# Moving the constants and pools of a float32r attention and feed-forward kernel so that TensorE's operands start at multiples of 128 bytes

## The chip, the cores and the metric

The kernel runs on one core of a Trainium2 chip. A core has five engines with queues of their own: TensorE (in the profile PE, with its weight loads as PEld), VectorE (DVE), ScalarE (ACT), GpSimd (POOL) and SyncE (SP). They share a memory of 128 partitions; a tile is a block of bytes at one offset in each of its partitions. TensorE multiplies a stationary operand (the weights, loaded by LDWEIGHTS) with a moving operand that is streamed column by column; both are read from this memory, and the product goes to the accumulators (PSUM). The metric is the device time in microseconds of one execution.

## The reference

Windowed causal attention over 8 batches of 8 heads, 576 positions, 64 elements each, and a feed-forward layer with a leaky activation on its output (4608 tokens, 512 -> 2048 -> 512), all in float32:

```python
rel = pos[:, None] - pos[None, :]
mask = (rel >= 0) & (rel < 64)
scores = np.where(mask, scale * np.matmul(q, k.transpose(0, 1, 3, 2)), -1000000000.0)
attn = np.exp(scores - np.max(scores, axis=-1, keepdims=True))
attn = attn / (np.sum(attn, axis=-1, keepdims=True) + 1e-09)
x = np.matmul(attn, v)          # then heads side by side: (4608, 512)
h = x @ w_in
g = np.maximum(h, 0.0) + alpha * np.minimum(h, 0.0)
return g @ w_out
```

The weights of the layer come as float64.

## The kernel before

Tokens are worked in 36 tiles of 128, in 13 blocks (`SIZES`: three of two tiles, ten of three). Per tile, attention computes scores (`s`, L490, full float32), a masked minimum and exponentials (DVE L504, ACT L512), a normalisation (POOL L529), a transpose (TensorE L553 in the opening, DVE L545 and L547 later) and the values (`av`, L577). The values are split into a high part `xh` and a low part `xl`, both of the type float32r (four bytes).

The layer runs in cells. Cell (n, f) is one block n and one slice f of 128 of the 2048 hidden features, 16 cells per block. `m_hidden` (L708 to L718) makes the hidden product from three split products of four matmuls each: `win_h` with `xh`, `win_h` with `xl`, `win_l` with `xh`. The weights are stationary; `xh` or `xl` moves, 384 columns wide in a block of three tiles and 256 in a block of two. Then come the slopes (ACT L724), the larger (DVE L730), the high part `gh` (ACT L737) and the low part `gl` (POOL L744). `m_add` (L749 to L762) adds to the output of each tile of the block: `gh` with `wout_h`, `gl` with `wout_h`, `gh` with `wout_l`. Here `gh` or `gl` is stationary (128 columns), and `wout_h` or `wout_l` moves, 512 columns wide. `o` of a cell is issued `LAG` = 2 cells after its `h`. So a cell of a three-tile block is 12 matmuls of 384 columns and 9 of 512.

The first three blocks are run by an order that `list_schedule` makes from estimated durations in `opening_graph`, because in that time the weights are still loaded and converted from float64 into high and low parts (DVE L389 to L416, ACT L394 and L433, POOL L422 and L437). From block 3 on the order is written out (L870 to L884), with attention for later blocks mixed in at two places of a block, for nine blocks (`attention_of`, called for blocks 3 to 11).

Nothing in either order depends on where a tile lies. Tiles are placed in the memory pool by pool in the order in which the pools are made (`const`, `io`, `wk`, `gp`), and inside `const` in the order of the calls of `const.tile`, each rounded up to 32 bytes. The first 1152 bytes of a partition (9 x 128) are taken before that. In `const` there stand first `ident` (512 bytes), `masks` (1536), `ebias` (4, rounded to 32), `alpha_rows` (512), `s_sb`, `s20_sb`, `s52_sb` (64 each), `ebias20` (32) and `sa_sb` (64): together 2880 bytes, 22.5 x 128. So `win_h` starts at byte 4032, 64 past a multiple of 128, and since `win_h` and all that follows it in `const` (`win_l`, `wout_h`, `wout_l`, two `pt`, `xh`, `xl`, `v`, `k`), in `io` (`raw`, `exp`, `val`) and at the head of `wk` (two `q`, two `w`) is a whole multiple of 128 long, they all start there: `wout_h` at 69568, `xh` at 143296, `w` at 206784. At the end of `wk` stand six small tiles of 32 bytes, 192 together, so that `gp` starts at 215168, a multiple of 128, and with it all of `g`, `gh` and `gl`. `ident` does too. Slices of these tiles that TensorE reads are offset by multiples of 128 bytes.

Of the kernel before, what the change touches and what calls it, by code (L numbers as in the profile page):

```python
# [9 lines left out]
F32 = mybir.dt.float32  # L10
F32R = mybir.dt.float32r
# [7 lines left out]
RING = 6  # L19
# [8 lines left out]
KRING = 3  # L28
# [144 lines left out]
def list_schedule(ops, slots, favour):  # L173
# [86 lines left out]
    v=(-24, -15, -188), vl=(26, -57, 103), xh=(211, 94, 23), xl=(-44, -6, 99),  # L260
# [26 lines left out]
def banded_attention_then_prelu_ffn(  # L287
# [15 lines left out]
    P = 128  # L303
    D = 64
    W = WINDOW
    KW = 2 * W
    C, T = qT.shape[0] * P, qT.shape[2] * P
    DFF = w_in.shape[1] // 2
    E = w_out.shape[1] // 2
    NP = C // P  # L310
    NF = DFF // P
# [8 lines left out]

    const = ctx.enter_context(tc.tile_pool(name="const", bufs=1))
    io = ctx.enter_context(tc.tile_pool(name="io", bufs=2))
    wk = ctx.enter_context(tc.tile_pool(name="wk", bufs=2))
    gp = ctx.enter_context(tc.tile_pool(name="gp", bufs=3))
    ps_o = ctx.enter_context(tc.tile_pool(name="ps_o", bufs=3, space=PSUM))
    ps_h = ctx.enter_context(tc.tile_pool(name="ps_h", bufs=2, space=PSUM))
    ps_a = ctx.enter_context(tc.tile_pool(name="ps_a", bufs=3, space=PSUM))


    ident = const.tile([P, P], F32, name="ident")  # L330
    nc.gpsimd.memset(ident, 1.0)
# [11 lines left out]

    for h in range(2):
        nc.gpsimd.memset(masks[h * W:(h + 1) * W, 1 + h, 0:W], NEG)
    ebias = const.tile([P, 1], F32, name="ebias")
    nc.vector.memset(ebias, -896.0 * 2**23)


# [7 lines left out]
    nc.vector.memset(ebias20, -916.0 * 2**23)  # L357
    sa_sb = const.tile([P, NF], F32, name="sa_sb")

    win_h = const.tile([P, NP, DFF], F32R, name="win_h")  # L360
    win_l = const.tile([P, NP, DFF], F32R, name="win_l")
    wout_h = const.tile([P, NF, E], F32R, name="wout_h")
    wout_l = const.tile([P, NF, E], F32R, name="wout_l")

# [71 lines left out]


    st = {}  # L440
    pts = [const.tile([P, 2, 2, 2, 2, W], F32, name=f"pt_{i}") for i in range(2)]
    xh = const.tile([P, NP, RING * P], F32R, name="xh")
    xl = const.tile([P, NP, RING * P], F32R, name="xl")
    tiles = [(n, i) for n, ts in enumerate(blocks) for i, t in enumerate(ts)]

    vring = const.tile([P, 2, 2 * KRING + 1, P], F32, name="v")
    kring = const.tile([P, 2, 2 * KRING + 1, 2, W], F32, name="k")

    def of_tile(t, name, shape):
        d = st.setdefault(t, {})  # L450
# [475 lines left out]
```

## Time and profile before

| | |
|---|---|
| median of the runs (3) | 921.17 us |
| lowest, highest | 920.11, 921.48 us |
| the profiled execution, its own time | 919.93 us |
| its span, first to last instruction | 917.9 us |
| granted TensorE clock over the span | 0.999 |
| bytes read from and written to the chip's main memory | 48.24 MB, 9.44 MB |

The page's second part, the span in 40 slices of 23 us, shows how the work is spread: the first row is TensorE, the others the engines that convert the weights and then accompany the cells; each digit is the busy share in tenths.

```profile
PE   9989999999999999999999999999999999999998
DVE  6999965236556455454454454454454445441111
ACT  6997767343453543543443443444344344332322
POOL 4899982233233332332333333333233233232221
```

The first six slices are the opening; after them DVE, ACT and POOL are half idle. The profile's durations of matmuls overlap: a matmul of 512 columns is listed with 397 ns (mean), while the next one starts well before that. Where the distance between matmuls matters, it has to be read from the starts in the timeline. Attribution of waits is inferred from semaphores.

### The profile page before, as it was taken

Reading aid. Unit: us, or ns where it says so; the run is one execution under the profiler, and the core shown is the slowest. Engines: PE = TensorE matmul, PEld = TensorE weight load, DVE = VectorE, ACT = ScalarE, POOL = GpSimd, SP = SyncE. Lnnn points to the kernel's source line nnn. Section 1 sums busy time; section 2 is a strip of 40 time slices with the busy share of each in tenths; the row PEclk is TensorE's granted clock in tenths of the full one; section 3 lists DMA queues with packets and bytes.
Section 4 is the critical chain, followed back from the end, with each engine's and each line's share of the span. In section 5 each row is a group of like instructions: output and inputs, shape, how many; then the busy total and the mean of one; then the engine's idle time right before and its main releaser. Section 6 shows DMA issues by size and latency. Waiting matters only on the chain.

```text
span 917.9 us, 18632 instructions
## 1 busy us (share of the span) xinstructions
PE 907.0 (99%) x7297; PEld 816.8 (89%) x7297; DVE 467.5 (51%) x1508; ACT 424.4 (46%) x1197; POOL 347.5 (38%) x350
## 2 busy tenths in 40 slices
PE   9989999999999999999999999999999999999998
PEld 8878888989999999999999999999999999999997
DVE  6999965236556455454454454454454445441111
ACT  6997767343453543543443443444344344332322
POOL 4899982233233332332333333333233233232221
PEclk9999999999999999999999999999999999999999
DMA  8655524020222013011110210210211200000000
GB/s 269 221 168 164 169 82 127 24 76 1 65 87 64 1 53 98 2 52 60 40 52 35 65 53 35 64 53 35 64 47 42 64 1 24 36 1 1 35 1 34
DMA packets 45606, 58.86 MB, mean 64 GB/s; under 512 B 2880, under 2 KB 38992, under 8 KB 45520
## 3 DMA queue, kind: packets, MB, share of 16 engines
q1 hardware_dynamic: 45056, 57.29, 19.6%
q8 instruction: 57, 0.93, 0.4%
q10 hardware_dynamic: 464, 0.40, 0.1%
q14 instruction: 29, 0.24, 0.1%
HBM read 48.24 MB, written 9.44 MB: 63 GB/s over the span
## 4 chain that ended last, share of the span: by engine, by line
PE 89%; DVE 6%; ACT 1%; issue 1%; POOL 1%; DMA 1%; DVEq 0%; ACTq 0%; POOLq 0%
PE h L717 40%; PE o L759 40%; PE s L490 4%; PE av L577 3%; DVE val L416 1%; DVE man L399 1%; PE warm L831 1%; DVE two L389 1%; DMA raw<-w_in 1%; DVE exp L410 1%; DVE w L504 1%; DVE g L730 1%; PE t L553 0%; POOL val L422 0%; ACT w L512 0%
## 5 line engine op out<-in xcount | busy, mean ns | idle before, releaser
L744 POOL TENSOR_TENSOR gl<-g,gh 128x384 fp32r<-128x384 f32 (+1 forms) x208 | 197.9, 952 | 507.9 <-ACT gh L737 444.0
L730 DVE SCALAR_TENSOR_TENSOR g<-h,s_sb,g 128x384 f32<-128x384 f32 (+1 forms) x208 | 121.9, 586 | 364.4 <-ACT g L724 364.2
L724 ACT ACTIVATE g<-h,sa_sb 128x384 f32<-128x384 f32 (+1 forms) x208 | 115.8, 557 | 324.9 <-PE h L717 320.1
L759 PE MATMUL o<-wout_h,gh 128*128 128x512 f32 x576 | 228.1, 397 | 0.5 <-ACT gh L737 0.4
L759 PE MATMUL o<-wout_h,gl 128*128 128x512 f32 x576 | 227.3, 395 | 0.5 <-POOL gl L744 0.5
L759 PE MATMUL o<-wout_l,gh 128*128 128x512 f32 x576 | 224.2, 390 | 0.0
L717 PE MATMUL h<-xh,win_h 128*128 128x384 f32 (+1 forms) x832 | 171.8, 328 | 3.1 <-DVE exp L410 1.9
L717 PE MATMUL h<-xl,win_h 128*128 128x384 f32 (+1 forms) x832 | 169.1, 324 | 0.0
L717 PE MATMUL h<-xh,win_l 128*128 128x384 f32 (+1 forms) x832 | 168.1, 323 | 0.0
L717 PEld LDWEIGHTS h<-xh,win_h 128*128 128x128 f32 x832 | 142.6, 188 | 22.4 <-DVE exp L410 4.0
L737 ACT CAST gh<-g 128x384 fp32r<-128x384 f32 (+1 forms) x208 | 101.6, 488 | 128.6 <-DVE g L730 116.3
L717 PEld LDWEIGHTS h<-xl,win_h 128*128 128x128 f32 x832 | 143.0, 188 | 0.2 <-DVE rc L521 0.2
L717 PEld LDWEIGHTS h<-xh,win_l 128*128 128x128 f32 x832 | 139.6, 188 | 0.2 <-issue 0.2
L759 PEld LDWEIGHTS o<-wout_l,gh 128*128 128x128 f32 x576 | 108.1, 188 | 23.7
L759 PEld LDWEIGHTS o<-wout_h,gh 128*128 128x128 f32 x576 | 107.9, 188 | 19.8 <-ACT xh L592 1.2
L759 PEld LDWEIGHTS o<-wout_h,gl 128*128 128x128 f32 x576 | 108.3, 188 | 15.9 <-POOL gl L744 1.2
L512 ACT ACTIVATE w<-w,nm 128x128 f32<-128x128 f32 x288 | 112.8, 394 | 5.2 <-DVE nm L504 5.0
L545 DVE STREAM_TRANSPOSE pt<-w 32x256 f32<-32x256 f32 x216 | 94.1, 436 | 5.9 <-POOL w L529 2.9
L529 POOL TENSOR_TENSOR w<-w,rc 128x512 f32<-128x512 f32 x65 | 66.5, 1042 | 48.4 <-DVE rc L521 33.1
L504 DVE CUSTOM_DVE_ANT_0 w<-s,masks 128x128 f32<-128x128 f32 x288 | 64.8, 285 | 7.1 <-PE s L490 7.1
L547 DVE STREAM_TRANSPOSE pt<-w 32x128 f32<-32x128 f32 x216 | 65.4, 303 | 4.2
L512 ACT ACTIVATION_READ_ACCUMULATOR w<-w,nm 128x1 f32 x288 | 54.4, 189 | 0.0
(52 smaller groups left out, 556.5 us busy)
## 6 DMA issues: line engine op xcount, KB each, us to landing
q<-qT SPq DMA_DIRECT2D x35, 256.0 KB, 3.5
out<-os SPq DMA_DIRECT2D x35, 256.0 KB, 2.2
raw<-w_in SPq DMA_DIRECT2D x16, 512.0 KB, 3.8
raw<-w_out SPq DMA_DIRECT2D x16, 512.0 KB, 3.5
k<-kT SPq DMA_DIRECT2D x24, 256.0 KB, 4.5
v<-vN SPq DMA_DIRECT2D x24, 256.0 KB, 4.2
v<-vN SPq DMA_DIRECT2D x12, 384.0 KB, 4.5
k<-kT SPq DMA_DIRECT2D x11, 384.0 KB, 4.4
```

Source lines behind the costliest of these rows:

```text
L490: nc.tensor.matmul(d["s"][a][x][us, 2 * a + h], q[r, a, h, us], kring[r, a, at + u:at + u + 2, h, :], start=True, stop=True)
L504: nc.vector.tensor_tensor_reduce(out=of_head(d["w"], g), in0=d["s"][e // 2][x][:, e].rearrange("p (b k) -> p b k", b=2), in1=mask.rearrang ...
L512: nc.scalar.activation(w, w, AF.Exp, scale=-1.0, bias=d["nm"][:, g:g + 1], accum_out=d["sm"][:, g:g + 1])
L529: nc.gpsimd.tensor_tensor(out=w, in0=w, in1=rc.unsqueeze(1).unsqueeze(3).broadcast_to(list(w.shape)), op=ALU.mult)
L545: nc.vector.transpose(to, w[:, x, j])
L547: nc.vector.transpose(to[:, :, j ^ 1], w[:, x, j, :, j ^ 1])
L717: nc.tensor.matmul(gs[n, f][:, :nt], wt[:, c, fs], xt[:, c, xs], start=(k == 0 and c == 0), stop=(k == 2 and c == NP - 1))
L724: nc.scalar.activation(g, ph[:, :nt], AF.Copy, scale=sa_sb[:, f:f + 1])
L730: nc.vector.scalar_tensor_tensor(out=g, in0=ph[:, :nt], scalar=s_sb[:, f:f + 1], in1=g, op0=ALU.mult, op1=ALU.max)
L737: nc.scalar.copy(gh, gs[n, f])
L744: nc.gpsimd.tensor_tensor(out=gl, in0=g, in1=gh.bitcast(F32), op=ALU.subtract)
L759: nc.tensor.matmul(po[t], g[of_g][:, ts], wt[:, f, :], start=(f == 0 and k == 0), stop=(f == NF - 1 and k == 2))
```

## The change

The large constants are allocated first in `const`, so that `win_h` starts at byte 1152 and each of the following at a multiple of 128; `ident` and `masks` come after them, at multiples of 128 too. `ebias` is made 24 elements long (96 bytes), of which the first is used, as before: with it `const` is 64 bytes longer, and `io` starts at 182272 = 1424 x 128. The pool `gp` is made ahead of `wk`, so that it starts at 202752 (a multiple of 128) and `wk` at 215040, with `q` and `w` at multiples of 128 and its small tiles last. What TensorE reads then lies at a multiple of 128 bytes; `alpha_rows` alone, read by one matmul, starts at 181472, 96 past one. Everything ends at byte 227520 of a partition, 64 further than before. No instruction is added, left out or reordered.

```diff
     const = ctx.enter_context(tc.tile_pool(name="const", bufs=1))
     io = ctx.enter_context(tc.tile_pool(name="io", bufs=2))
+    gp = ctx.enter_context(tc.tile_pool(name="gp", bufs=3))
     wk = ctx.enter_context(tc.tile_pool(name="wk", bufs=2))
-    gp = ctx.enter_context(tc.tile_pool(name="gp", bufs=3))
...
+    win_h = const.tile([P, NP, DFF], F32R, name="win_h")
+    win_l = const.tile([P, NP, DFF], F32R, name="win_l")
+    wout_h = const.tile([P, NF, E], F32R, name="wout_h")
+    wout_l = const.tile([P, NF, E], F32R, name="wout_l")
+    pts = [const.tile([P, 2, 2, 2, 2, W], F32, name=f"pt_{i}") for i in range(2)]
+    xh = const.tile([P, NP, RING * P], F32R, name="xh")
+    xl = const.tile([P, NP, RING * P], F32R, name="xl")
+    vring = const.tile([P, 2, 2 * KRING + 1, P], F32, name="v")
+    kring = const.tile([P, 2, 2 * KRING + 1, 2, W], F32, name="k")
 
     ident = const.tile([P, P], F32, name="ident")
...
-    ebias = const.tile([P, 1], F32, name="ebias")
+    ebias = const.tile([P, 24], F32, name="ebias")[:, :1]
     nc.vector.memset(ebias, -896.0 * 2**23)
...
-    win_h = const.tile([P, NP, DFF], F32R, name="win_h")
-    win_l = const.tile([P, NP, DFF], F32R, name="win_l")
-    wout_h = const.tile([P, NF, E], F32R, name="wout_h")
-    wout_l = const.tile([P, NF, E], F32R, name="wout_l")
...
-    pts = [const.tile([P, 2, 2, 2, 2, W], F32, name=f"pt_{i}") for i in range(2)]
-    xh = const.tile([P, NP, RING * P], F32R, name="xh")
-    xl = const.tile([P, NP, RING * P], F32R, name="xl")
...
-    vring = const.tile([P, 2, 2 * KRING + 1, P], F32, name="v")
-    kring = const.tile([P, 2, 2 * KRING + 1, 2, W], F32, name="k")
```

## The prediction

> **What bounds the kernel.** I read the page first: the span, the busy shares, the chain of work that ended last.
>
> ```profile
> span 917.9 us, 18632 instructions
> PE 907.0 (99%) x7297; PEld 816.8 (89%) x7297; DVE 467.5 (51%) x1508; ACT 424.4 (46%) x1197; POOL 347.5 (38%) x350
> PE 89%; DVE 6%; ACT 1%; issue 1%; POOL 1%; DMA 1%; DVEq 0%; ACTq 0%; POOLq 0%
> ```
>
> TensorE is busy 99% of the span and carries 89% of the chain; no other engine is above 51%. But a busy TensorE says nothing of how fast its matmuls follow each other, and the 6% of DVE lies somewhere. So I asked for the last conversion of the weights (the low parts, L437), and for the busy time on either side of its end.
>
> ```profile
> L437 POOL TENSOR_TENSOR wout_l<-val,wout_h x16: 1287/1299/1326, 25.8 to 130.6; 128x512 fp32r<-128x512 f32 x16
> 132.00:917.90 785.90, 781.79 (x6094) 707.42 (x6092) 352.34 (x1207) 321.17 (x923) 233.86 (x235) 1.00 0.14 44
> ```
>
> The second row's columns are the window, its length, then busy time and count of PE, PEld, DVE, ACT, POOL, then granted clock, DMA share, GB/s. The last low part starts at 130.6 us and takes 1.3, so the weights are all there at 132 us. From then on TensorE is busy for 781.8 of 785.9 us at a granted clock of 1.00. There is no wait to remove after 132 us: only shorter matmuls make that stretch shorter. Before it, the conversions on DVE and POOL set the pace as much as TensorE does.
>
> Next, the distance from one matmul to the next. The durations in the groups (397 ns for a 512-column one) are latencies that overlap, so I took starts from the timeline of TensorE: a cell near the end, a cell of the 256-column blocks, and the 27 `o` matmuls of the tail (first and last).
>
> ```profile
> 851.43 0.87 PE L717 MATMUL h<-xh,win_h 128*128 128x384 f32 x4
> 852.13 0.86 PE L717 MATMUL h<-xl,win_h 128*128 128x384 f32 x4
> 852.84 0.86 PE L717 MATMUL h<-xh,win_l 128*128 128x384 f32 x4
> 853.53 0.39 PE L759 MATMUL o<-wout_h,gh 128*128 128x512 f32 x1
> ```
> ```profile
> 172.03 0.64 PE L717 MATMUL h<-xh,win_h 128*128 128x256 f32 x4
> ...
> 173.46 0.39 PE L759 MATMUL o<-wout_h,gh 128*128 128x512 f32 x1
> ```
> ```profile
> 907.70 0.39 PE L759 MATMUL o<-wout_h,gh 128*128 128x512 f32 x1
> ...
> 913.65 0.39 PE L759 MATMUL o<-wout_l,gh 128*128 128x512 f32 x1
> ```
>
> The first number of a row is its start. 384 columns: (853.53 - 851.43) / 12 = 175.0 ns each. 256 columns: (173.46 - 172.03) / 12 = 119.2 ns. 512 columns: (913.65 - 907.70) / 26 = 228.8 ns. From 256 to 512 columns that is 109.6 ns more for 256 columns, 0.428 ns per column, so 119.2 - 109.7 = 9.5 ns remain that don't depend on the columns; the 384 come out at 174.0 by this line and measured 175.0. **Each matmul pays some 10 ns beyond its columns.**
>
> Now the addresses. What these matmuls stream (`xh`, `xl`, `wout_h`, `wout_l`) starts at 64 past a multiple of 128 bytes in every one of them, since each slice is offset by whole multiples of 512 bytes from bases that all end that way. Read in pieces of 128 bytes (32 columns of four bytes), 256, 384 and 512 columns that start in the middle of a piece touch 9, 13 and 17 pieces in place of 8, 12 and 16. And 119.2 / 9 = 13.2, 175.0 / 13 = 13.5, 228.8 / 17 = 13.5 ns: one price fits three lengths within 2%. That is why I take the surplus for one piece too many, read once per matmul.
>
> **The change, part by part.** No instruction is added, removed or reordered: the same tiles in another order of allocation, and `ebias` 92 bytes longer. So the change acts only through addresses.
>
> *The `h` and `o` matmuls.* All four streamed operands come to a multiple of 128, and each matmul touches one piece fewer: 119.2 x 8/9 = 106.0, 175.0 x 12/13 = 161.5, 228.8 x 16/17 = 215.4 ns; it saves 13.2, 13.5 and 13.5 ns. I count only those after 132 us:
>
> ```profile
> 132.00:917.90 785.90, 388.46 (x2116) 365.55 (x2114) 1.00 0.14 44
> ```
> ```profile
> 132.00:917.90 785.90, 386.89 (x1554) 287.36 (x1554) 1.00 0.14 44
> ```
> ```profile
> L717 PE MATMUL h<-xh,win_h 128*128 128x384 f32 x640 | 139.2, 339 | 0.0
> ```
>
> The first row is of L717 alone (`h`), the second of L759 alone (`o`); the third says that each of the three `h` products has 640 of 384 columns, 1920 in all, so 2116 - 1920 = 196 of the counted ones have 256. Sum: 1554 x 13.5 + 1920 x 13.5 + 196 x 13.2 ns = 21.0 + 25.9 + 2.6 = **49.5 us**.
>
> By the Trainium skill, TensorE: Matmul & The Clock Gate, section "Wait — 56ns, not 53.3ns?", a warm back-to-back matmul costs N / 2.4 GHz plus about 2.5 ns, 215.7 ns at 512 columns. The trace's 228.8 is 13 ns above that, which the page does not explain; with its figures as the floor the sum would be an estimated 46 us in place of 49.5.
>
> *The matmuls before 132 us* (`h`, then `o`):
>
> ```profile
> 0.00:132.00 132.00, 52.54 (x383) 48.53 (x384) 1.00 0.58 182
> ```
> ```profile
> 0.00:132.00 132.00, 46.32 (x174) 30.63 (x174) 1.00 0.58 182
> ```
>
> These 557 would save some 13.3 ns each as well, 7.4 us, but a TensorE that is faster there comes earlier to the next converted slice and waits for it. The cover is the work of DVE and POOL that ends with the row of L437 above. Value 0; without the cover, 7 us more.
>
> *The attention matmuls and transposes* (full float32; `k`, `q`, `pt`, `v`, `w` move too). For these I looked at the opening:
>
> ```profile
> 11.43 1.95 PE L831 MATMUL warm<-ident 128*128 128x128 f32 x16
> 13.21 0.60 PE L553 MATMUL t<-ident,w 128*128 128x128 f32 x4
> 13.65 0.61 PE L831 MATMUL warm<-ident 128*128 128x128 f32 x4
> 14.10 0.60 PE L553 MATMUL t<-ident,w 128*128 128x128 f32 x4
> 14.53 0.61 PE L831 MATMUL warm<-ident 128*128 128x128 f32 x4
> ```
>
> Transposes stream `ident` (at a multiple of 128 already) and take (0.44 + 0.43) / 8 = 109 ns for 128 columns. At two steps of 0.428 ns a column, which is how I read full float32, that is 109.6: nothing is left for a cost per matmul. It speaks against a fixed cost of changing weights. At half speed a surplus piece also has time to arrive unseen, so I take 0 here. The other end:
>
> ```profile
> 8.51 1.10 PE L490 MATMUL s<-k,q 64*64 64x128 f32 x32
> 9.55 1.60 PE L831 MATMUL warm<-ident 128*128 128x128 f32 x12
> ```
> ```profile
> L490 PE MATMUL s<-k,q 64*64 64x128 f32 x1152 | 39.9, 275 | 0.0
> ...
> L577 PE MATMUL av<-pt,v 64*64 64x64 f32 x1152 | 29.6, 218 | 0.0
> L577 PE MATMUL av<-pt,v 64*64 64x128 f32 x576 | 29.2, 273 | 0.5 <-ACT pt L562 0.5
> ```
>
> 32 score matmuls of 128 columns take 1.04 us, 32 ns each, so nearly four run side by side; a piece per group of four is 2880 / 4 x 13.4 ns = 9.6 us of gain at most.
>
> *The other engines.* `raw`, `val`, `w` and the weights move by 64 bytes under DVE, ACT, POOL and the DMAs; `g`, `gh` and `gl` stay at multiples of 128. POOL's subtraction runs over both kinds:
>
> ```profile
> L744 POOL TENSOR_TENSOR gl<-g,gh 128x384 fp32r<-128x384 f32 x160 | 162.4, 1015 | 477.1 <-ACT gh L737 413.3 <-PE o L759 63.8
> L744 POOL TENSOR_TENSOR gl<-g,gh 128x256 fp32r<-128x256 f32 x48 | 35.6, 743 | 30.8 <-ACT gh L737 30.7
> L437 POOL TENSOR_TENSOR win_l<-val,win_h 128x512 fp32r<-128x512 f32 x16 | 20.8, 1299 | 2.5 <-ACT win_h L433 2.4
> ```
>
> From 743 and 1015 ns, 512 columns at multiples of 128 would be 1287; at 64 past them they took 1299, 1% more. Over 64 POOL instructions of the conversions that is 0.8 us either way: value 0. DMA holds 1% of the chain, 9 us, all in the opening; I take 0 of it, and an end of the range covers some.
>
> *What is late next.* After an `h` come the slopes, the larger, the high and the low part, and `o` follows two cells behind (LAG = 2).
>
> ```profile
> L724 ACT ACTIVATE g<-h,sa_sb 128x384 f32<-128x384 f32 x160 | 93.1, 582 | 313.3 <-PE h L717 313.3
> L730 DVE SCALAR_TENSOR_TENSOR g<-h,s_sb,g 128x384 f32<-128x384 f32 x160 | 98.8, 618 | 337.7 <-ACT g L724 337.6
> L737 ACT CAST gh<-g 128x384 fp32r<-128x384 f32 x160 | 82.2, 514 | 109.6 <-DVE g L730 109.6
> ```
>
> With POOL's 1015 that is 582 + 618 + 514 + 1015 ns = 2.7 us, and two cells shrink from 2 x 4.16 to 2 x 3.88 us (12 x 161.5 + 9 x 215.4 ns): a margin of 5 us remains, less in the cells that also hold attention.
>
> **Sum.** The profiled execution took 919.9 us itself (span 917.9 and 2.0 around it): 919.9 - 49.5 = 870.4. The median shown is 1.2 us above that execution, so the forecast is **872 us**. Its own range: 862 if the attention gains its 9.6 us as well or the opening its 7, 882 if a fifth of the saving stays away.
>
> **Rivals.**
>
> *No change, 921 us.* The 10 to 13 ns are a fixed cost of a four-byte matmul at one column per step (a change of weights, the start of a stream) and not a piece. The same three lengths fit, since N + 32 columns and one more piece are the same numbers here: no `h` or `o` of this kernel starts anywhere else, so the trace can't part them directly. Against it stands the transpose, which changes weights every time and shows no such cost; but it runs at half speed, which may hide it. By the Trainium skill, SBUF — State Buffer, "Specifications (TRN2)", lines are 16 bytes long, and by that a start at 64 is on a line already and this rival holds; no row here shows a 16-byte step.
>
> *A small gain, 911 us.* The `h` of the last quad (852.84 to 853.53) take 172.5 ns, 13.3 per piece; at that price an `o` would be 225.6, and it is 228.8. The `o` are those whose weights (`gh`, `gl`) start at a multiple of 128 while the stream doesn't. If only this mixture costs, the change saves 9 x 3.2 ns, and the 30 ns by which the cell's first two quads (0.70 and 0.71 us) are over the last, about 59 ns a cell: 160 cells, 9.4 us.
>
> *The gain is partly eaten, 883 us.* In the 18 places where attention is mixed in (two in each of nine blocks), the two cells of margin are 0.6 us shorter; if each lost all of it, 18 x 0.6 = 11 us come back. Against it: after 132 us TensorE waits for nearly nothing, so the margins there are not used up.
>
> *Slower, 930 us.* With everything at multiples of 128, weights and stream start at the same place in their pieces. The trace has that in `warm` alone (`ident` on both sides): (13.21 - 11.43) / 16 = 111.2 ns, 2.5 more than the transposes, where the weights `w` start at 64. If that is a collision, and the stream saves nothing, 3670 matmuls after 132 us lose 2.5 ns each, 9.2 us. It decides from 0.5 ns per matmul without a saved piece (below that, 1.8 us, it can't be told); with one, only above 13.5.
>
> **How the numbers follow.** About 0.2% is what a measurement of this kernel can tell from no change. Forecast 0.60; partly eaten 0.06; small gain 0.08; no change 0.17; slower 0.09. Faster by over 0.2%: 0.60 + 0.06 + 0.08 = 0.74; within: 0.17; slower: 0.09. The range has to take in no change to leave out no more than 2 in 10: 862 to 922 leaves the slower case and the tails.
>
> **What would show it.** In the timeline of TensorE the last 26 steps of `o` should be 215 ns each and the 12 `h` of a cell 1.94 us in place of 2.10; conversions should still end near 132 us, with longer waits of TensorE before. If steps stay at 229 and 175, no piece was saved; if they shrink and the span doesn't, a wait after 132 us must have appeared; if `h` and `o` shrink by different amounts, the piece is not the unit.

## The result

The changed kernel takes **926.1 us** in the median (925.56 to 926.69) against 921.1 before (920.11 to 921.48): a ratio of 1.0056, 95% interval 1.0043 to 1.0069. It is slower by 5.0 us, where 49 us less were forecast.

The page of the changed kernel first: the span, the busy shares, the chain by engine.

```profile
span 923.9 us, 18632 instructions
PE 913.1 (99%) x7297; PEld 818.8 (89%) x7297; DVE 467.5 (51%) x1508; ACT 424.1 (46%) x1197; POOL 346.8 (38%) x350
PE 90%; DVE 6%; ACT 1%; POOL 1%; issue 1%; DMA 1%; ACTq 0%; DVEq 0%; POOLq 0%
```

All the growth is busy time of TensorE, 907.0 to 913.1 us; DVE, ACT and POOL are within 0.7 us of before, with the same counts. So no wait was added: the matmuls themselves follow each other more slowly. (Spans of single executions scatter by more than medians: run e11 below has a span of 919.5 us at a median equal to that of the kernel before, whose span is 917.9. Of the 6.0 us by which the two spans here differ, 1.2 had arisen before the first block of three tiles starts, at 189 us.)

The chain of work in order of time shows which matmuls. Columns: start, length, line, count. First the end of the kernel before, then of the changed one (its line numbers are 2 higher).

```profile
903.70 2.06 PE o L759 x9
905.75 2.11 PE h L717 x12
907.86 6.19 PE o L759 x27
```
```profile
909.70 2.09 PE o L761 x9
911.78 2.11 PE h L719 x12
913.90 6.28 PE o L761 x27
```

The 12 `h` of a cell take 2.11 us in both: to stream from a multiple of 128 bytes saved nothing at all. The 9 `o` went from 2.06 to 2.09 us. From the starts of the timeline, averaged over the 138 cells of three-tile blocks with no attention in them, `h` takes 2.106 us before and 2.108 after, `o` 2.061 and 2.090, a cell 4.167 and 4.198. 31 ns by 160 cells are 5.0 us: the whole loss of the medians. One cell of the changed kernel, step by step:

```profile
854.24 0.86 PE L719 MATMUL h<-xh,win_l 128*128 128x384 f32 x4
854.93 0.39 PE L761 MATMUL o<-wout_h,gh 128*128 128x512 f32 x1
855.16 0.39 PE L761 MATMUL o<-wout_h,gl 128*128 128x512 f32 x1
855.39 0.39 PE L761 MATMUL o<-wout_l,gh 128*128 128x512 f32 x1
855.62 0.39 PE L761 MATMUL o<-wout_h,gh 128*128 128x512 f32 x1
855.85 0.40 PE L761 MATMUL o<-wout_h,gl 128*128 128x512 f32 x1
856.09 0.40 PE L761 MATMUL o<-wout_l,gh 128*128 128x512 f32 x1
856.33 0.40 PE L761 MATMUL o<-wout_h,gh 128*128 128x512 f32 x1
...
857.02 0.87 PE L719 MATMUL h<-xh,win_h 128*128 128x384 f32 x4
```

No single wait is responsible: each `o` starts 0.23 us after the one before, and a few 0.24 (the step from 856.09 to 856.33, the sixth of the nine, is 240.8 ns on average in these cells, against 225.8 before). The 27 `o` of the tail have the same slow steps: 6.28 against 6.19 us. In the middle of that tail, from 916.87 to 918.80 us of the changed kernel, DVE, ACT, POOL and the DMAs are idle, and steps of 233 and 240 ns stand there too. So it is TensorE with its two operands, and no other engine is needed for it.

### The profile page after: what moved, and what is told of

Read it like the earlier page. It is cut to its first block, busy times and chain, and to the rows that moved or that the text cites. A ratio compares the mean times of both kernels' runs of the same rounds, so it can differ in the third digit from the quotient of the medians.

```text
span 923.9 us, 18632 instructions
## 1 busy us (share of the span) xinstructions
PE 913.1 (99%) x7297; PEld 818.8 (89%) x7297; DVE 467.5 (51%) x1508; ACT 424.1 (46%) x1197; POOL 346.8 (38%) x350
## 4 chain that ended last, share of the span: by engine, by line
PE 90%; DVE 6%; ACT 1%; POOL 1%; issue 1%; DMA 1%; ACTq 0%; DVEq 0%; POOLq 0%
PE o L761 41%; PE h L719 41%; PE s L492 4%; PE av L579 3%; PE warm L833 1%; DVE val L423 1%; DVE two L396 1%; DVE man L406 1%; DVE exp L417 1%; DVE w L506 1%; DVE g L732 1%; PE t L555 1%; DMA raw<-w_in 1%; POOL val L429 0%; ACT w L529 0%
## 5 line engine op out<-in xcount | busy, mean ns | idle before, releaser
L761 PE MATMUL o<-wout_l,gh 128*128 128x512 f32 x576 | 228.1, 397 | 0.0
```

The source lines that it names most:

```text
L761: nc.tensor.matmul(po[t], g[of_g][:, ts], wt[:, f, :], start=(f == 0 and k == 0), stop=(f == NF - 1 and k == 2))
```

## The experiments

`o` has its weights (`gh`, `gl`) in one pool and its stream (`wout`) in another. The change moved both, and with them the distance between the two. That of `h` it did not change: `win` and `xh` moved together, and `h` had both operands at the same place modulo 256 before the change too. In what follows a distance is the address of the weights less that of the stream.

**One part of the change at a time.** The first two runs undo the move of `gp`, and do that move alone:

```diff
 # e1_large_first: the change, with the pools as before
-    gp = ctx.enter_context(tc.tile_pool(name="gp", bufs=3))
     wk = ctx.enter_context(tc.tile_pool(name="wk", bufs=2))
+    gp = ctx.enter_context(tc.tile_pool(name="gp", bufs=3))
 # e2_gp_first: the kernel before, with the pools as in the change
+    gp = ctx.enter_context(tc.tile_pool(name="gp", bufs=3))
     wk = ctx.enter_context(tc.tile_pool(name="wk", bufs=2))
-    gp = ctx.enter_context(tc.tile_pool(name="gp", bufs=3))
```

> The change without its move of the pool gp: the streamed operands at multiples of 128 bytes, gh and gl (the stationary operands of o) at 64 past one. Theory 'together' (an o matmul is slower where its stationary and its streamed operand start at the same place of a 128-byte piece; before they were 64 apart): o steps back to 229 ns, a cell of 12 h and 9 o in 4.167 us, about 921 us. Rival 'stream at a multiple' (a streamed operand that starts at a multiple of 128 is the slower one, whatever the stationary one does): o steps of 232 ns, a cell in 4.198 us, about 926 us. Rival 'pool' (gp's new place, ahead of wk, is what costs): 921 us, like 'together'; the next run parts these.

> The kernel before with the pool gp ahead of wk alone: everything that streams stays 64 past a multiple of 128, and gh and gl come there too. 'Together': o steps of 232 ns, a cell in 4.198 us, about 926 us. 'Stream at a multiple': o steps of 229 ns, a cell in 4.167 us, about 921 us. 'Pool': 926 us with the first run at 921 would fit as well; then the o steps have to be the slow ones in both kernels that have gp first whatever the offsets, which the third and fourth run vary.

Measured: e1 925.7 us, ratio to before 1.0051 (1.0034 to 1.0067), `o` 2.100 us, `h` 2.100; e2 923.4 us, ratio 1.003 (1.0018 to 1.0041), `o` 2.081 us, `h` 2.105. The chain of e1, then of e2:

```profile
910.65 2.10 PE o L761 x9
912.75 2.10 PE h L719 x12
914.85 6.32 PE o L761 x27
```
```profile
907.19 2.08 PE o L759 x9
909.27 2.10 PE h L717 x12
911.37 6.18 PE o L759 x27
```

Each part alone makes the kernel slower, and all three theories fell: "together" wanted 921 us for e1, "stream at a multiple" 921 us for e2, and "pool" 921 us for e1. Four arrangements gave four values of `o`: 2.061, 2.090, 2.100, 2.081. Modulo 256 bytes their distances are 192 (gh at 218240, wout_h at 69568), 128, 64 and 0.

**Other starts at the same and at another distance.**

```diff
 # e3_h_apart: 64 bytes between the weights and xh (and ebias short again, so that the pools stay put)
     wout_l = const.tile([P, NF, E], F32R, name="wout_l")
+    const.tile([P, 16], F32, name="pad")
     pts = [const.tile([P, 2, 2, 2, 2, W], F32, name=f"pt_{i}") for i in range(2)]
-    ebias = const.tile([P, 24], F32, name="ebias")[:, :1]
+    ebias = const.tile([P, 1], F32, name="ebias")
 # e4_all_at_32: the change, 32 bytes further
+    const.tile([P, 8], F32, name="pad")
     win_h = const.tile([P, NP, DFF], F32R, name="win_h")
```

> The change with 64 bytes more ahead of pt, xh, xl, v and k: now h streams from 64 past a multiple of 128 with its weights at a multiple, o has both at a multiple as in the change. 'Together': o stays at 232 ns; h, which had both operands at the same place before and after, has them apart for the first time, so its 12 steps in a cell (2.107 us before, 2.108 after) should change if the same mechanism acts there, by up to the 0.05 us that they are above 12 x 173.3. 'Stream at a multiple': h as before, 2.107. Of the prediction's step (a piece of 128 bytes too many) nothing is left if h is the same from 0 and from 64.

> The change with 32 bytes more ahead of everything, so that all that TensorE reads starts 32 past a multiple of 128, streams and weights together. 'Together': o steps of 232 ns and a cell in 4.198 us, as in the change. 'Stream at a multiple' (of 128): o steps of 229 ns. If TensorE reads in pieces of 64 bytes, this kernel reads one piece more than both others: 16 columns, 6.7 ns more per matmul, a cell in 4.31 us or more, about 940 us. If the surplus of some 32 columns per matmul is fixed, h steps stay at 175.6 ns on average.

Measured, the chain of e3 first, then that of e4:

```profile
905.61 2.09 PE o L762 x9
907.70 2.09 PE h L720 x12
```
```profile
909.47 2.09 PE o L762 x9
911.56 2.11 PE h L720 x12
```

e4 is the change step by step: `h` 2.108 us, `o` 2.090 us, 925.8 us in one timed execution. Where things start doesn't matter, from 0 to 32, as long as the distances stay. In e3 `h` came down to 2.085 us: the first change of its distance (0 to 192 modulo 256) moved it by 23 ns, more than the 8 ns by which it had moved in e1 without one. Of its steps the second to the eleventh are within 1 ns of 173.3, where before the first six went up to 185; only the first and the last, at the borders to `o`, are longer. `o` kept distance 128 and about its time, 2.094. The one timed execution took 921.9 us.

**Sixteen distances in one execution.** Weights laid out slice by slice with a gap, so that the distance grows with f:

```diff
 # e5_sweep_32 (in e6_sweep_4 the gap is 1 element in place of 8)
-    win_h = const.tile([P, NP, DFF], F32R, name="win_h")
-    win_l = const.tile([P, NP, DFF], F32R, name="win_l")
-    wout_h = const.tile([P, NF, E], F32R, name="wout_h")
-    wout_l = const.tile([P, NF, E], F32R, name="wout_l")
+    win = const.tile([P, NF, 2 * NP * P + 8], F32R, name="win")
+    win_h, win_l = (win[:, :, i * NP * P:(i + 1) * NP * P].rearrange("p f (c q) -> p f c q", c=NP) for i in range(2))
+    wout = const.tile([P, NF, 2 * E + 8], F32R, name="wout")
+    wout_h, wout_l = (wout[:, :, i * E:(i + 1) * E] for i in range(2))
...
-            nc.tensor.matmul(gs[n, f][:, :nt], wt[:, c, fs], xt[:, c, xs],
+            nc.tensor.matmul(gs[n, f][:, :nt], wt[:, f, c], xt[:, c, xs],
```

> The change with the weights laid out slice by slice (win as 16 rows of high and low part, wout likewise) and 32 bytes between the slices, so that the distance between where the weights and the stream of a matmul start grows by 32 bytes from one f to the next: for h 0, 32, ... 480 (modulo 512), for o 384, 352, ... down to 416 again. One execution then holds 16 distances, each in ten three-tile blocks. Theory 'distance' (the surplus of an o or h beyond some fixed part depends on the distance between its two operands modulo 512, not on where either lies): the cell of the same f takes the same time in all blocks, different f differ by up to 50 ns, and among them the known ones return: o of 2.061 us at 192, 2.081 at 0, 2.090 at 384, 2.100 at 64. Rival 'place' (what counts is where one operand lies by itself): no pattern in f, or one that does not give those values.

> The same with 4 bytes between the slices: the distance for h goes through 384, 388, ... 444 and for o through 448, 444, ... 388, and the slices start at all multiples of 4. 'Distance' with a fine grain (a bank or line of 16 bytes or less): a pattern in f. With a grain of 32 or 64 bytes: two or three groups of f. If a stream that starts off a 64-byte line had to read one line more, h steps would rise from 173 to 180 ns for most f.

The chain of e5 in the last block, around `h` of f = 6 and around `h` of f = 14 (the `o` after it is two slices behind):

```profile
872.33 2.08 PE h L717 x12
874.41 2.05 PE o L759 x9
876.46 2.12 PE h L717 x12
878.58 2.10 PE o L759 x9
...
905.85 2.08 PE h L717 x12
907.92 2.05 PE o L759 x9
909.98 2.12 PE h L717 x12
```

Eight slices apart, 256 bytes, the times return. Medians over the blocks, of cells with no attention in them, from the starts of the timeline, in ns (f and f + 8 beside each other; distances modulo 256):

```
distance     0          32         64         96         128        160        192        224
h, 12      2108 2108  2094 2093  2095 2095  2085 2085  2104 2103  2112 2118  2081 2081  2116 2116
o, 9       2052 2052  2093 2091  2102 2102  2109 2109  2089 2089  2098 2098  2081 2081  2096 2096
```

The known values return for `o` at 128 (2.090 in the change) and 64 (2.100 in e1), but not at 0 (2.081 in e2) and 192 (2.061 before). So the distance is right but it is not all: which steps are slow seems to depend on the `h` around as well, which has other distances here (e9 below tests it). The whole execution took 924.2 us. With 4 bytes (e6, 927.9 us) `h` lies between 2.086 and 2.149 and `o` between 2.070 and 2.152 us; all four slices in which `o` takes 2.148 to 2.152 have their stream start at 4 bytes past a multiple of 16 (and so their distance 12 past one; the run can't part the two). At 8 and 12 bytes past a multiple of 16 `o` takes 2.070 to 2.114 us, no more than at a multiple, 2.073 to 2.105. Its chain, around the `o` of f = 5 and of f = 9, two of the four:

```profile
879.90 2.15 PE h L717 x12
882.05 2.15 PE o L759 x9
884.20 2.11 PE h L717 x12
886.32 2.08 PE o L759 x9
...
896.75 2.13 PE h L717 x12
898.88 2.15 PE o L759 x9
```

No distance of these sweeps brought `h` below 2.081 us, 173.4 ns a step: the surplus that doesn't depend on the columns is left untouched.

**Distances chosen.** From the sweep, 192 for `h` and 0 for `o`; then the change with nothing but the distance of `o` put back.

```diff
 # e8_distances: e3 with
-    ebias = const.tile([P, 1], F32, name="ebias")
+    ebias = const.tile([P, 33], F32, name="ebias")[:, :1]
 # e11_distance_back: the change with
-    ebias = const.tile([P, 24], F32, name="ebias")[:, :1]
+    ebias = const.tile([P, 40], F32, name="ebias")[:, :1]
```

> Two distances chosen from the sweep of 32 bytes, modulo 256: from the streamed to the stationary operand 192 for h (xh and xl 64 past a multiple of 128, win at a multiple) and 0 for o (gp 128 bytes further than in the third run). 'Distance modulo 256': h of 2.082 us and o of 2.054 us as in the slices f = 6 and 14 of the sweep, a cell of 4.14 us against 4.167 before and 4.198 after the change; 160 cells x 0.03 us less than before, about 916 us. Rival 'history' (the low sums of the sweep came from the neighbours with other distances): a cell of 4.16 us or more, 920 us or more.

> The change with ebias 64 bytes longer once more: streams at multiples of 128 as in the change, gh and gl at 64 past one as in the first run, but the distance for o is 192 modulo 256, as in the kernel before (the first run has 64, the change 128). 'Distance modulo 256': o steps of 229 ns, 2.061 us, a cell of 4.167 us, about 921 us: the whole loss of the change gone, with every stream at a multiple of 128. Rival 'place modulo 128': as the first run, o of 2.100 us, a cell of 4.200 us, about 926 us.

Measured: e8 **914.6 us, ratio 0.9929 (0.9915 to 0.9943)**, faster than both kernels; e11 921.0 us, ratio 0.9998 (0.9989 to 1.0008). The chain of e8, then of e11:

```profile
898.80 2.05 PE o L762 x9
900.85 2.08 PE h L720 x12
902.93 6.15 PE o L762 x27
```
```profile
905.24 2.06 PE o L761 x9
907.30 2.11 PE h L719 x12
909.40 6.19 PE o L761 x27
```

e8: `h` 2.081, `o` 2.052, a cell 4.133 us; 160 x (4.167 - 4.133) = 5.4 of the 6.5 us, for the rest there is no sum: the two-tile blocks have a part, as their `h` steps went from 120 to 118 ns, and executions differ by some 1 us. e11, with `h` 2.106, `o` 2.061 and a cell of 4.167 us, is the kernel before, step by step, although every large stream starts at a multiple of 128 and `gh` and `gl` at 64 past one, as in e1. From the change to e11 nothing moves but `io`, `gp`, `wk` and a few small constants, all by 64 bytes; the distance of `o` goes from 128 to 192. One address by itself can't be it: `wout_h` lies at 128 modulo 256 in the change, in e1 and in e11, with three values of `o`, and `gh` at 192 in e1 and in e2, with two. The kernel before and e11, or the change and e4, have the distance in common at other addresses, and each pair agrees step by step. **This shows the distance to be the cause of the loss.**

To see how much is distance and how much is history, `h` was held at 192 and `o` swept again:

> The third run's 192 for h, and for o a sweep of 32 bytes per f: 128, 96, ... down to 160 (modulo 256), each twice in 16 slices. 'Distance modulo 256': o of slice f and of slice f + 8 agree within a few ns, the lowest at 0 with 2.054 us, 2.09 at 128, 2.06 at 192; h stays at 2.085 us for all. Rival 'history': h follows the o before it.

In e9 (e3 with the gap of 8 elements in `wout` alone; 921.2 us) `o` took, at distances 0 to 224 in steps of 32, the same for f and f + 8: 2058, 2094, 2090, 2095, 2095, 2097, 2075 and 2085 ns. The period of 256 holds; 0 is the best again; but 192 gives 2.075 after this `h` and 2.061 after the `h` of before. And `h`, at one distance throughout, did not stay at 2.085 us as expected: it ran from 2.078 to 2.095 with the `o` around it. Both theories have a part, the distance the larger one (39 ns in `o` against 17 in `h`).

**What the fixed surplus is.** Three runs, of one timed execution each, on the 13 ns that the prediction had taken for a piece too many. e7 leaves out 96 of the 128 columns of ten of the twelve weights of an `h`; e10 and e12 work `h` with fewer digits.

```diff
 # e7_narrow_weights
+                m = P if (k, c) in ((0, 0), (2, NP - 1)) else 32
-                nc.tensor.matmul(gs[n, f][:, :nt], wt[:, c, fs], xt[:, c, xs],
+                nc.tensor.matmul(gs[n, f][:m, :nt], wt[:, c, f * P:f * P + m], xt[:, c, xs],
 # e10_bf16_view
+                wb, xb = (x.bitcast(mybir.dt.bfloat16).rearrange("p (n t) -> p n t", t=2)[:, :, 1]
+                          for x in (wt[:, c, fs], xt[:, c, xs]))
-                nc.tensor.matmul(gs[n, f][:, :nt], wt[:, c, fs], xt[:, c, xs],
+                nc.tensor.matmul(gs[n, f][:, :nt], wb, xb,
 # e12_bf16_dense: e8 with
-    win_h = const.tile([P, NP, DFF], F32R, name="win_h")
+    win_h = const.tile([P, NP, DFF], BF16, name="win_h")
...
-    xh = const.tile([P, NP, RING * P], F32R, name="xh")
+    xh = const.tile([P, NP, RING * P], BF16, name="xh")
 # (win_l and xl likewise, and the two subtractions read them as bfloat16)
```

> The change with 10 of the 12 matmuls of each h reduced to 32 stationary columns (they fill 32 of the 128 partitions of h; the rest of these products is left out), the streams unchanged. If the fixed surplus of about 32 columns per matmul comes with the loading of the weights beside the stream, the h steps fall from 175 towards 162 ns, 10 x 11 ns per cell, some 18 us in all. If it belongs to the stream itself, they stay at 173 ns and the time at 925 us.

> The change with the h matmuls reading the upper two bytes of each value as bfloat16, from the same addresses at the same spacing of four bytes (h is then a product of shortened values). If the surplus of some 32 columns per matmul belongs to the four-byte type, the h steps of 384 columns fall from 173 to some 162 ns or less, 0.13 us per cell. If it belongs to the change from one matmul to the next whatever the type, or to the bytes that the stream spans, they stay at 173 ns.

> The eighth run (distance 0 for o kept) with win, xh and their low parts stored as bfloat16, so that h streams two bytes a column without gaps (its products keep fewer digits than float32r); o is unchanged and is the comparison within the run. If the surplus of 32 columns that is left at the best distances belongs to streams of four bytes a column, the h steps of 384 columns fall from 173.3 towards 162.5 ns while o stays at 226.7: 0.13 us less per cell, some 20 us in all. If it comes with every change of weights, h stays at 173.

e7 (922.1 us): the groups by form show what became of a weight load, the timeline what became of the steps.

```profile
L720 PEld LDWEIGHTS h<-xl,win_h 128*32 128x32 f32 x832 | 89.7, 108 | 44.9 <-DVE rc L523 0.2
```
```profile
904.57 0.86 PE L720 MATMUL h<-xl,win_h 128*32 128x384 f32 x4
905.27 0.86 PE L720 MATMUL h<-xh,win_l 128*32 128x384 f32 x4
```

The loads fell from 188 to 108 ns, but the four steps still take 0.70 us, 175 ns each; `h` sums to 2.093 us. The length of the weight load is not the surplus. (The sum moved by 15 ns at the same addresses, so narrower weights do alter the pattern.)

e10 (913.7 us): steps of 169 ns, 4 less than 173.3, not 11. So two-byte values at the old spacing lose only a part of the surplus. e12 (897.9 us) changes the spacing too. Its timeline:

```profile
879.69 0.82 PE L721 MATMUL h<-xh,win_h 128*128 128x384 bf16 x4
880.35 0.81 PE L721 MATMUL h<-xl,win_h 128*128 128x384 bf16 x4
881.00 0.81 PE L721 MATMUL h<-xh,win_l 128*128 128x384 bf16 x4
881.52 0.53 PE L763 MATMUL o<-wout_h,gh 128*128 128x512 f32 x1
881.88 0.39 PE L763 MATMUL o<-wout_h,gl 128*128 128x512 f32 x1
882.11 0.40 PE L763 MATMUL o<-wout_l,gh 128*128 128x512 f32 x1
```

From 880.35 to 881.00 four steps of 384 columns take 0.65 us, 162.5 ns each, and so they are in all cells; in the two-tile blocks 256 columns take 109.1 ns. `o`, left in float32r in the same execution, stays at 0.23 us (from 881.88 to 882.11); to the nanosecond its steps are 232 ns on average after the first, 4 more than in e8 at the same distance. With that the cell came down by 85 ns and not by the 130 expected. By the Trainium skill, TensorE: Matmul & The Clock Gate, section "Wait — 56ns, not 53.3ns?", a step is N / 2.4 GHz + 2.5 ns, which is 162.5 and 109.2: the trace agrees, with 162.5 and 109.1, for two-byte operands without gaps. For float32r it doesn't: at the column time that e12's two lengths give, (162.5 - 109.1) / 128 = 0.417 ns, 173.3 ns are the time of 384 + 32 columns, and no distance gave a mean step below 173.2. So dense two-byte operands are rid of 11 of the 13 ns, and with float32r the surplus was there at each start that was tried (0, 32 and 64 past a multiple of 128). Whether the stream or the weights bring it, this run can't say, as it changed both.

## Why the prediction was wrong

- **What bounds the kernel: right.** TensorE alone; all of the 5 us came as its busy time, and a wait appeared nowhere.
- **A surplus of some 10 ns per matmul that doesn't depend on the columns: right**, 13.3 ns for 384 and 512 columns at the best distances, some 11 for 256.
- **"I take the surplus for one piece too many": the step that failed.** It fitted three lengths within 2%, but N + 32 columns fit as well, and the prediction said that the trace could not part the two. `h` from 0, 32 and 64 past a multiple of 128 has the same floor of 173.3 ns. The term "`h` and `o`, 49.5 us" was 0 for `h` and had the wrong sign for `o`.
- **"Nothing is left for a cost per matmul" in the transposes: true and misleading.** It was the ground on which the fixed cost was put at 0.17. The 0.428 ns per column behind it held slow `o` steps; at the 0.417 of e12 two steps a column are 106.7 ns, and some 2 of the 109 are left. That is still far from 13, but the transposes are full float32 at two steps a column, and a cost that belongs to float32r at one step a column need not show there; the prediction named that escape and gave it too little.
- **No effect on other engines, the opening and the attention: right** within what these runs tell.
- **"No instruction is reordered, so the change acts only through addresses": right, but it looked at each address by itself.** The distance between the two operands of one matmul was not considered for `o`, and there it changed from 192 to 128 modulo 256: 3.2 ns more for each of the 9 `o` of a cell, 31 ns with what `h` adds, 160 cells.
- The rivals: "no change" had the account of `h` right. "Slower" had the nearest mechanism, weights against stream, but drawn from `warm` against the transposes it would have hit `h` and `o` alike with 2.5 ns, 9.2 us. It said that the trace had weights and stream at the same place in `warm` alone; `h` had the two at one place as well, both 64 past a multiple of 128, so for `h` the change made nothing new in this. Measured were 5.0 us, nearly all in `o`, and distance 0, the supposed collision, is the best place for `o` (2.052 us in e8). "Small gain" saw that `o` was dear for its columns and took a common start for the cure. The range ended at 922 us because the case "slower" was among those left out.

What stays open: why the period is 256 bytes, and what in TensorE's reading makes the pattern (the runs show that it needs no other engine and that narrower weights alter it); and which of the two four-byte operands costs the 32 columns. Nor do the runs tell whose stream counts. By the trace a load starts with the matmul before its own (before the change, the load for the `o` of 851.20 us and the `o` ahead of it both at 850.97), so the stream beside it is that matmul's. Within the `h` and within the `o` of a cell both streams have the same distance; where the two meet they need not, which may be the part that the history has.

## What to carry to other kernels

When a step time fits "one unit too many", look for a case in the trace where the unit is absent before building a sum on it; a fixed cost of the same size fits just as well. In a TensorE-bound kernel with float32r, moving tiles by some tens of bytes changed the time by 0.6% for the worse and 0.7% for the better, through the distance between the weights and the stream modulo 256 bytes: sweep it in one execution by a gap between slices, pick the distances, and then measure them held constant. If the digits allow it, two-byte operands saved more here than any placing (11 ns of each 173; 897.9 us in one execution against 914.6).

## What the runs showed of the hardware

- Float32r: the step from one matmul of N columns to the next was N + 32 columns of 0.417 ns for 384 and 512 columns at best (173.3 and 226.7 ns, e8) and 118 to 120 ns for 256, bfloat16 without gaps 162.5 ns for 384 and 109.1 for 256 (e12), bfloat16 at a spacing of four bytes 169 for 384 (e10).
- Beyond that floor up to 70 ns in 12 `h` and over 100 in 9 `o` (e6) depend on the distance modulo 256 bytes (e5, e9, e11) and on the matmuls around (e9). The `o` of one slice repeat it within 4 ns from block to block.
- By the Trainium skill, SBUF — State Buffer, "Specifications (TRN2)", lines are 16 bytes long; e6 agrees in part only: the streams that start 4 bytes past a multiple of 16 were the slowest (2.15 us for nine `o`), those that start 8 or 12 past one were no slower than those at a multiple (2.07 to 2.11 us).
